# Softmax weights and tokens turned by transposing transfers of 16-bit halves instead of TensorE

## The chip, the cores and the metric

The kernel runs on one core of one Trainium2 chip. Its engines are called as in the profile: PE (TensorE, the matmuls; PEld is its weight load), DVE (VectorE), ACT (ScalarE), POOL (GpSimd) and SP (SyncE, which issues every transfer here). The metric is the time of one execution on the device in microseconds (us). Three runs of the kernel before took 473.75, 475.15 and 475.65 us, so the median is 475.15 us.

## The reference

Sparse attention over 4 batches, 8 heads, 768 positions and 64 channels is followed by a mixing block on the joined heads (512 channels). All data is 32-bit float.

```python
def _attn_ref(q, k, v):
    block, window = (32, 16)
    k_sum = k.reshape(B, H, nb, block, D).max(axis=3)       # 24 block keys
    v_sum = v.reshape(B, H, nb, block, D).mean(axis=3)      # 24 block values
    scores_l = scale * q @ k.T           # kept where |i - j| < 16
    scores_s = scale * q @ k_sum.T + log(block)
    a = softmax(concatenate([scores_l_m, scores_s]))
    return a @ concatenate([v, v_sum])

def _moe_ref(x, w_theta, w_tok_r, w_tok_i, w_ch):
    theta = x @ w_theta
    zr, zi = x * cos(theta), x * sin(theta)
    y = w_tok_r @ zr + w_tok_i @ zi      # over the positions of a batch
    u = x + y
    return u + maximum(u @ w_ch, 0.0)
```

## The kernel before

Each batch has six tiles of 128 positions. For one tile, `att_tile` multiplies queries with 24 block keys and 94 neighbouring keys for each of two groups of 64 queries (118 scores a row, L1609). `att_half`, called twice for four heads each, takes the maximum on DVE (L1622), the exponential on ACT (L1626), turns the four 128x118 blocks of weights on PE into PSUM (L1629, tile `p`), copies them to SBUF (`pt`, by the helper at L1466) and multiplies them with the values (L1635, tile `av`). DVE or ACT divides by the sums into `xn`, which holds a tile of tokens by position.

`turn_tile` then turns the four 128x128 blocks of `xn` on PE (L1657, tile `t`), copies them to their place in `x`, which holds the turned tokens of a whole batch, and splits them in a leading part `xh` (L1466) and a rest `xl` (L1472), since PE multiplies in a shorter format, three products for one. `theta_tile` multiplies with `w_theta` (L1689) and takes cosine and sine (L1697 to L1712); products with the tokens go to `w` and `zb`, split into `zq`. When a batch has its six tiles, `mix_step` adds up the token mixing in two halves `h` of six steps `s`: for batch 0 at L1732, after that at L1767. At the last step DVE adds `x` to the sums in place (L1778) and the result `u` goes to DRAM (`u_scratch`). After all batches the pools of the attention are given back, and `out_unit` loads `u`, splits it, multiplies with `w_ch` (L1809) and stores the output.

The weights come as halves of 64-bit numbers that `load_f64` converts on ACT, DVE and POOL while batch 0 runs (L1513 to L1522).

The order of everything is written out in the table ORDER: the letters name the engine (P, A, V, G, S for PE, ACT, DVE, POOL, SP) and the numbers are steps from one recorded operation to the next. Each engine works through its own part of the list in order and waits for what an operation reads and for its buffers. SP issues all transfers in this order too, so that one that waits holds those behind it. Attention of a batch is interleaved with the mixing of the batch before. Buffers that matter here: `xn` has 2, `pt` 1, `e` 2, the values `v` 4, `x` 2.

Of the kernel before, what the change touches and what calls it, by code (L numbers as in the profile page):

```python
# [1913 lines left out]
```

## Time and profile before

| | |
|---|---|
| median of three runs | 475.15 us |
| the profiled execution | 473.4 us |
| its span, first to last instruction | 471.6 us |
| PE busy | 452.2 us, 96% |
| DVE busy | 326.2 us, 69% |
| ACT busy | 267.0 us, 57% |
| POOL busy | 125.9 us, 27% |
| moved by transfers | 62.16 MB, 132 GB/s in the mean |

All numbers of the trace are from the one profiled execution; 1.8 us of its time lie outside the span. Busy is the time in which an engine worked on at least one instruction, so the durations of instructions that overlap add up to more than it. Matmuls overlap by their drain: how long one kept PE is read from its start to the next start.

### The profile page before, as it was taken

The numbers are of one execution on the slowest core, as the hardware profiler recorded it, in microseconds if no ns is written. First come the engines' busy times: TensorE is split into PE (matmuls) and PEld (weight loads), VectorE is DVE, ScalarE is ACT, GpSimd is POOL, SyncE is SP. The second block draws the span as 40 slices with busy tenths as digits, with TensorE's granted clock in tenths as the row PEclk, the third lists the DMA queues.
The fourth block names the chain that finished last, engine by engine and source line by source line (L and its number), as shares of the span: only waits on it lengthen the run. The fifth ranks groups of instructions, "written<-read, shape, count | busy, mean of one in ns | idle before, by whom it ended". The sixth has DMA issues, their size and how long they took to land.

```text
span 471.6 us, 10324 instructions
## 1 busy us (share of the span) xinstructions
PE 452.2 (96%) x3904; PEld 384.5 (82%) x3904; DVE 326.2 (69%) x999; ACT 267.0 (57%) x568; POOL 125.9 (27%) x160
## 2 busy tenths in 40 slices
PE   2999899999999999999999899999999999999997
PEld 1487667778888888888888688888888889999996
DVE  5899999999899776747668665434756695333354
ACT  2499999977588785736467846647754230010010
POOL 3235453434133122132123332322110220130310
PEclk9999999999999999999999999999999999999999
DMA  8988645334116351251082204020101651473663
GB/s 318 363 276 286 222 153 170 99 122 124 58 34 199 122 158 45 71 179 33 21 286 78 75 1 125 22 70 2 35 24 44 208 161 68 133 247 110 207 200 121
DMA packets 34226, 62.16 MB, mean 132 GB/s; under 512 B 3968, under 2 KB 16000, under 8 KB 34176
## 3 DMA queue, kind: packets, MB, share of 16 engines
...
HBM read 48.90 MB, written 12.58 MB: 130 GB/s over the span
## 4 chain that ended last, share of the span: by engine, by line
PE 80%; ACT 6%; DVE 5%; DMA 3%; issue 3%; POOL 1%; SPq 1%; ACTq 0%; POOLq 0%; DVEq 0%
PE m L1767 29%; PE c L1809 14%; PE t L1689 11%; PE m L1732 8%; PE av L1635 5%; PE p L1629 4%; PE s L1609 4%; PE t L1657 2%; PE m L1497 2%; PE av L1548 1%; DVE f L1522 1%; ACT e L1626 1%; SPq L1463 1%; ACT pt L1466 1%; ACT L1711 1%
## 5 line engine op out<-in xcount | busy, mean ns | idle before, releaser
L1767 PE MATMUL m<-wt,zq 128*128 128x512 f32 x864 | 162.2, 340 | 0.0
L1767 PEld LDWEIGHTS m<-wt,zq 128*128 128x128 f32 x864 | 133.3, 188 | 17.9
L1626 ACT ACTIVATE e<-e,st 128x118 f32<-128x118 f32 x192 | 66.6, 389 | 14.5 <-DVE st L1622 13.2
L1809 PE MATMUL c<-cuh,wth 128*128 128x384 f32 x256 | 65.7, 338 | 0.0
L1689 PE MATMUL t<-wth,xh 128*128 128x512 f32 x192 | 61.4, 401 | 0.0
L1732 PE MATMUL m<-wt,zq 128*128 128x512 f32 (+1 forms) x288 | 56.8, 344 | 0.1
L1622 DVE CUSTOM_DVE_ANT_0 e<-s,cs 128x118 f32<-128x118 f32 x192 | 46.3, 272 | 11.9 <-PE p L1629 6.5
L1732 PEld LDWEIGHTS m<-wt,zq 128*128 128x128 f32 x288 | 43.9, 189 | 7.1 <-DVE zq L1472 0.7
L1466 ACT CAST cuh<-cu 128x384 fp32r<-128x384 f32 x19 | 9.5, 513 | 68.2 <-DMA cu<-u_scratch 65.6
L1809 PEld LDWEIGHTS c<-cuh,wth 128*128 128x128 f32 x256 | 45.9, 188 | 0.5
L1809 PE MATMUL c<-cul,wth 128*128 128x384 f32 x128 | 43.3, 338 | 0.2 <-DVE cul L1472 0.2
L1814 DVE SCALAR_TENSOR_TENSOR cu<-c,cu 128x384 f32<-128x384 f32 x32 | 17.5, 554 | 34.4 <-PE c L1809 24.2
L1635 PEld LDWEIGHTS av<-v,pt 118*64 118x64 f32 x768 | 27.0, 137 | 17.1 <-issue 9.0
L1472 POOL TENSOR_TENSOR zq<-w,zq 128x512 fp32r<-128x512 f32 x14 | 19.4, 1387 | 73.3 <-ACT zq L1466 43.1
L1689 PEld LDWEIGHTS t<-wth,xh 128*128 128x128 f32 x192 | 33.5, 188 | 6.7 <-issue 0.5
L1689 PE MATMUL t<-wth,xl 128*128 128x512 f32 x96 | 37.8, 394 | 0.0
L1635 PE MATMUL av<-v,pt 118*64 118x65 f32 x768 | 33.6, 227 | 3.7 <-DMA v<-vg 2.5
L1697 ACT ACTIVATE w<-t,bmagic 128x512 f32<-128x512 f32 x24 | 16.5, 686 | 32.2 <-PE t L1689 20.7
L1629 PE MATMUL p<-cs,e 128*118 128x128 f32 x192 | 30.4, 281 | 0.9 <-ACT e L1626 0.9
L1472 POOL TENSOR_TENSOR zq<-zb,zq 128x512 fp32r<-128x512 f32 (+1 forms) x19 | 22.9, 1211 | 27.0 <-ACT zq L1466 20.1
L1472 POOL TENSOR_TENSOR cul<-cu,cuh 128x384 fp32r<-128x384 f32 x14 | 15.1, 1094 | 55.8 <-ACT cuh L1466 33.1
L1472 POOL TENSOR_TENSOR xl<-x,xh 128x512 fp32r<-128x512 f32 x11 | 14.4, 1310 | 53.8 <-DVE xh L1466 33.1
...
## 6 DMA issues: line engine op xcount, KB each, us to landing
...
q<-qg SPq DMA_DIRECT2D x24, 256.0 KB, 3.9
cu<-u_scratch SPq DMA_DIRECT2D x32, 192.0 KB, 2.8
out<-cu SPq DMA_DIRECT2D x32, 192.0 KB, 2.0
...
u_scratch<-x SPq DMA_DIRECT2D x16, 256.0 KB, 3.7
wt<-wtr SPq DMA_DIRECT2D x6, 512.0 KB, 6.3
wt<-wti SPq DMA_DIRECT2D x6, 512.0 KB, 7.2
```

The lines of the kernel that those rows point to most:

```text
L1472: op(f"VG tt {n}", lambda e: V[e].tensor_tensor(dst(), src(), hi().bitcast(F32), op=ALU.subtract), reads, writes)
L1609: mm("s" if len(parts) == 1 else "s0", [lambda p=p, g=g, h=h, c=c, kk=kk: nc.tensor.matmul(sc[h].get()[ROW[g], p, c], q.get()[ROW[h], p, R ...
L1622: op("V ttr", lambda eng, n=n: nc.vector.tensor_tensor_reduce(e.get()[:, n], sc[n % 2].get()[:, 2 * a + n // 2], mask(m), -SCALE, 3.0e38, ...
L1626: op("A exp", lambda eng, n=n: nc.scalar.activation(e.get()[:, n], e.get()[:, n], AF.Exp, bias=st.get()[:, n:n + 1], scale=-1.0), [(st, n) ...
L1629: mm("tr", [lambda n=n: nc.tensor.transpose(tp.get()[:NK, n], e.get()[:, n], ident()) for n in range(NH)], [e, (cs, "ident")], [tp])
L1635: mm("av", [lambda n=n, g=g: nc.tensor.matmul(xa.get()[ROW[g], n], t.get()[:, n, ROW[g]], v[g].get()[:NK, NH * a + n], start=True, stop=Tr ...
L1689: calls = [lambda t=t, xx=xx, k=k, c=c: nc.tensor.matmul(th.get(), xx.get()[:, c], w_th[c].get()[:, k], start=(c == 0 and t == 0), stop=(c ...
L1697: op(f"A psumb {DM}", lambda e: nc.scalar.activation(r(), th.get(), AF.Identity, bias=bmagic.get(), scale=1.0 / TWO_PI), [th, bmagic], [R])
L1732: nc.tensor.matmul(acc, zk(k, r, c), w_t[s, r, th].get()[:, kw], start=(clear and s == r == t == 0), stop=(s == NT - 1 and r == 1 and t == ...
L1767: nc.tensor.matmul((ma[c].get(), half(2, c)())[th], zk(k, r, c), w_t[s, r, th].get()[:, kw], start=(s == r == t == 0 and (th == 0 or c == 0)),
L1809: calls = [lambda t=t, k=k, uu=uu, c=c, co=co, acc=acc: nc.tensor.matmul(acc.get(), w_ch[c].get()[:, k, co * P:(co + 1) * P], uu.get()[:, ...
L1814: op(f"V ttp {HT}", lambda e, co=co, acc=acc: nc.vector.scalar_tensor_tensor(u.get()[:, co], acc.get(), 0.0, u.get()[:, co], ALU.max, ALU. ...
```

## The change

From tile `DT` = 6 on, that is for batches 1 to 3, the turning matmuls and the copies out of PSUM give way to `turn_words`: a copy parts the 32-bit numbers in two planes of 16 bits (`un`, the operation called part), one transposing transfer on SP's queue turns 128 rows of 1024 such halves, eight blocks of 128x128, from SBUF to SBUF (`ut`), and a second copy joins the halves (join). Either copy may go to POOL, ACT or DVE. For the softmax weights, 118 wide, the ten columns that fill a block up are zeroed first. Batch 0 is turned by PE as before.

The turned tokens have no buffer for a whole batch any more. Each tile of `x` is stored to `u_scratch` (512 runs of 512 bytes), loaded again in `mix_step` as `ux`, added to and stored a second time. Eight buffers `zx` of 2 KB a partition serve `un`, `ut`, the tile of tokens and the first loads of values; `ux` has four. ORDER is new from end to end; one line of it stands for the rest.

```diff
-S+98
+S+104
...
-TUNE = dict(XT=1, XB=2, WB=1, TB=1, XNB=2, XHB=2, FB=2, FC=2, QB=2, VB=4, KN=2, ZQ=8, ZS=11, EB=2, PC=4, WU=40)
+TUNE = dict(XT=1, WB=1, TB=1, XNB=2, XHB=2, FB=2, FC=2, QB=2, VB=4, KN=2, ZQ=8, ZB=11, ZX=8, UX=4, DT=6, EB=2, PC=4, WU=40)
...
+    def turn_words(n, w, src, reads, dst, writes):
+        un = Ref(tpool, [P, 2, n, P], U16, tag="zx", bufs=K["ZX"])
+        ut = Ref(tpool, [P, 2, n, P], U16, tag="zx", bufs=K["ZX"])
+        if w < P:
+            op("GV set 1", lambda e: V[e].memset(un.get()[..., w:], 0), [], [(un, "pad")])
+        op(f"GAV part {2 * n * w}", lambda e: copy(e, un.get()[..., :w], src().bitcast(U16).rearrange("p n (w k) -> p k n w", k=2)),
+           reads, [(un, "data")])
+        op("S turn 128 2048", lambda e: nc.sync.dma_start(
+            ut.get().rearrange("p k n t -> p (k n) t"), un.get().rearrange("p k n w -> p (k n w)"), transpose=True), [un], [ut])
+        op(f"GAV join {2 * n * P}", lambda e: copy(e, dst().bitcast(U16).rearrange("w n (t k) -> w k n t", k=2), ut.get()[:w]), [ut], writes)
...
-        tp = bank("p", [P, NH, P])
-        mm("tr", [lambda n=n: nc.tensor.transpose(tp.get()[:NK, n], e.get()[:, n], ident()) for n in range(NH)],
-           [e, (cs, "ident")], [tp])
         t = Ref(apool, [NK, NH, P], tag="pt", bufs=K["TB"])
-        op(f"AV psum {NH * P}", lambda e: copy(e, t.get(), tp.get()[:NK]), [tp], [t])
+        if b * NT + i < K["DT"]:
+            tp = bank("p", [P, NH, P])
+            mm("tr", [lambda n=n: nc.tensor.transpose(tp.get()[:NK, n], e.get()[:, n], ident()) for n in range(NH)],
+               [e, (cs, "ident")], [tp])
+            op(f"AV psum {NH * P}", lambda e: copy(e, t.get(), tp.get()[:NK]), [tp], [t])
+        else:
+            turn_words(NH, NK, e.get, [e], t.get, [t])
...
+        x = Ref(tpool, [P, NC, P], tag="zx", bufs=K["ZX"])
...
+        else:
+            turn_words(NC, P, lambda: xn[b, i].get().rearrange("p h d -> p (h d)").rearrange("p (c d) -> p c d", d=P), [xn[b, i]], x.get, [x])
+        hi_op(x_h.get, x.get, DM, [x], [x_h])
+        lo_op(x_l.get, x.get, x_h.get, DM, [x, x_h], [x_l])
+        dma(lambda: u_dram[b][:, :, i * P:(i + 1) * P].rearrange("c p t -> p c t"), x.get, NC * P, P * 4, [x], [("ud", (b, i))])
...
+                u = Ref(tpool, [P, 512], tag="ux", bufs=K["UX"])
+                part, row = (lambda u=u, n=n: u.get()[:, :n]), (lambda th=th, ch=ch: u_dram[b, ch][:, TT[th]])
+                dma(part, row, P, n * 4, [("ud", (b, t)) for t in range(i0, i0 + n // P)], [u])
+                op(f"V ttp {n}", lambda e, part=part, acc=acc: nc.vector.tensor_tensor(part(), acc(), part(), op=ALU.add), [areg], [u])
+                dma(row, part, P, n * 4, [u], [("ur", (b, ch, th))])
```

Three places show what moves. The first is DVE at the end of batch 0's mixing, where it adds the tokens to the last sums (L1778 before, L1848 now; `m` is a bank of sums, L1622 and L1684 are the maxima). Before, the last of batch 0's additions is its instruction 443, with 88 maxima ahead of it:

```order
L1648 TENSOR_TENSOR xn_2182<-av_2077,st_1837 128x256
L1778 TENSOR_TENSOR x_400<-m2_1595,x_400 128x256
L1622 ISA e_2059,st_2060<-s1_1954,cs_170 128x118
L1622 ISA st_2060 128x1
L1778 TENSOR_TENSOR x_400<-m1_1472,x_400 128x256
L1778 TENSOR_TENSOR x_400<-m0_1516,x_400 128x512
L1560 TENSOR_REDUCE vt_2221<-f_2196 128x16
L1778 TENSOR_TENSOR x_400<-m1_1472,x_400 128x256
```

Now it is instruction 494, with 97 maxima ahead of it:

```order
L1706 RECIPROCAL st_2037<-st_2037 128x4
L1713 TENSOR_TENSOR xn_2347<-av_2369,st_2037 128x256
L1610 TENSOR_REDUCE vt_2016<-f_2390 128x8
L1610 TENSOR_REDUCE vt_2016<-f_2357 128x16
L1516 CAST zq_2414<-w_2255 128x512
L1684 ISA e_2423,st_2424<-s1_2330,cs_120 128x118
L1684 ISA st_2424 128x1
L1848 TENSOR_TENSOR ux_2426<-m1_1712,ux_2426 128x256
```

DVE has 51 more instructions ahead of that addition than before. The second place is PE at the last tile of the last batch, where its tokens are turned and multiplied with `w_theta`. Before, PE turns them (`t` from `xn`) in the midst of the mixing:

```order
L1767 MATMUL m0_4533<-wt200_1060,zq_4557 128x512
L1767 MATMUL m2_4534<-wt201_1702,zq_4557 128x256
L1657 MATMUL t_4710<-cs_170,xn_4675 128x128 x4
L1767 MATMUL m1_4576<-wt110_856,zq_4374 128x512
L1767 MATMUL m2_4534<-wt111_1529,zq_4374 128x256
```

Now mixing goes on to the first theta matmul of that tile, which reads `xh` and `xl`:

```order
L1835 MATMUL m0_4608<-wt300_734,zq_4755 128x512
L1835 MATMUL m2_4609<-wt301_1830,zq_4755 128x256
L1835 MATMUL m0_4608<-wt300_734,zq_4805 128x512
L1835 MATMUL m2_4609<-wt301_1830,zq_4805 128x256
L1757 MATMUL t_4849<-wth0_80,xh_4821 128x512 x2
L1757 MATMUL t_4849<-wth0_80,xl_4834 128x512
```

The turn has left PE's list; between the tile's last product with the values and this theta matmul PE has 12 mixing matmuls, the 12 theta matmuls of the tile before and 18 more mixing matmuls. The third place is SP in the attention of the last batch, with loads of queries and values (`q`, `v`) and stores of `u`. Before:

```order
L1463 DMA u_scratch<-x_1651 128x512
L1463 DMA v_3737<-vg 96x520
L1463 DMA q_4103<-qg 128x512
L1463 DMA q_4124<-qg 128x512
L1463 DMA v_3674<-vg 96x520
L1463 DMA v_3665<-vg 96x520
L1463 DMA v_3737<-vg 96x520
```

Now (`zx` from `zx` is a turn, `u_scratch` from `zx` the store of a turned tile):

```order
L1513 DMA v_3750<-vg 96x520
L1674 DMA_TRANSPOSE zx_4519<-zx_4444 128x8x128
L1674 DMA_TRANSPOSE zx_4524<-zx_4459 128x8x128
L1513 DMA v_3616<-vg 96x520
L1513 DMA v_3799<-vg 96x520
L1674 DMA_TRANSPOSE zx_4604<-zx_4535 128x8x128
L1674 DMA_TRANSPOSE zx_4668<-zx_4549 128x8x128
L1513 DMA u_scratch<-ux_4425 128x512
L1513 DMA u_scratch<-ux_4264 128x256
L1674 DMA_TRANSPOSE zx_4691<-zx_4551 128x8x128
L1674 DMA_TRANSPOSE zx_4742<-zx_4698 128x8x128
L1513 DMA u_scratch<-zx_4633 128x4x128
```

The turns stand in the same queue as the loads of values, which wait behind them.

## Rows read from the trace of the kernel before

**Rows 1.** The head of the profile's page: the span, and each engine's busy time, its share of the span and its instructions.

```profile
span 471.6 us, 10324 instructions
PE 452.2 (96%) x3904; PEld 384.5 (82%) x3904; DVE 326.2 (69%) x999; ACT 267.0 (57%) x568; POOL 125.9 (27%) x160
```

**Rows 2.** The chain that ended last, its shares of the span by engine.

```profile
PE 80%; ACT 6%; DVE 5%; DMA 3%; issue 3%; POOL 1%; SPq 1%; ACTq 0%; POOLq 0%; DVEq 0%
```

**Rows 3.** Busy time of each engine (and its instructions) in stretches of the span, in us; behind them the granted clock, the share of the DMA engines and GB/s.

```profile
core 0: us, PE busy (x) PEld busy (x) DVE busy (x) ACT busy (x) POOL busy (x), PEclk, DMA share, GB/s
0.00:30.00 30.00, 20.68 (x216) 12.68 (x217) 22.62 (x75) 13.91 (x30) 9.54 (x15) 1.00 0.91 316
30.00:60.00 30.00, 27.43 (x440) 21.86 (x441) 29.13 (x99) 29.09 (x64) 13.34 (x13) 1.00 0.80 269
60.00:100.00 40.00, 38.30 (x283) 29.21 (x282) 38.72 (x112) 37.08 (x77) 15.87 (x24) 1.00 0.45 141
100.00:148.00 48.00, 48.00 (x468) 41.40 (x468) 43.33 (x152) 34.85 (x83) 15.55 (x23) 1.00 0.30 96
148.00:154.00 6.00, 6.00 (x75) 5.03 (x74) 5.86 (x14) 4.64 (x14) 1.65 (x2) 1.00 0.53 176
154.00:340.00 186.00, 183.67 (x1669) 155.29 (x1668) 117.31 (x416) 119.65 (x246) 47.18 (x66) 1.00 0.27 83
```

**Rows 4.** The timeline of PE in a piece of batch 2: start in us, duration in us, engine, line, operation, output from input. `p` from `cs,e` are turns of softmax weights, `t` from `cs,xn` turns of tokens, `m` the mixing, `t` from `wth` the theta matmuls (12 of them from 212.64 us to 215.50).

```profile
204.31 0.65 PE L1629 MATMUL p<-cs,e 128*118 128x128 f32 x4
204.72 4.43 PE L1767 MATMUL m<-wt,zq 128*128 128x512 f32 x24
209.08 0.69 PE L1635 MATMUL av<-v,pt 118*64 118x65 f32 x16
...
210.66 0.65 PE L1629 MATMUL p<-cs,e 128*118 128x128 f32 x4
211.15 0.60 PE L1657 MATMUL t<-cs,xn 128*128 128x128 f32 x4
211.51 1.29 PE L1767 MATMUL m<-wt,zq 128*128 128x512 f32 x6
212.64 0.69 PE L1689 MATMUL t<-wth,xh 128*128 128x512 f32 x2
...
215.50 0.73 PE L1767 MATMUL m<-wt,zq 128*128 128x512 f32 x3
```

**Rows 5.** Groups of instructions by line, engine, operation and shape: count, busy us, mean ns of one, and the idle time of the engine before them with what ended it.

```profile
L1626 ACT ACTIVATE e<-e,st 128x118 f32<-128x118 f32 x192 | 66.6, 389 | 14.5 <-DVE st L1622 13.2 <-DVE st L1641 0.6
...
L1622 DVE CUSTOM_DVE_ANT_0 e<-s,cs 128x118 f32<-128x118 f32 x192 | 46.3, 272 | 11.9 <-PE p L1629 6.5 <-PE s L1609 4.8 <-issue 0.5
...
L1635 PE MATMUL av<-v,pt 118*64 118x65 f32 x768 | 33.6, 227 | 3.7 <-DMA v<-vg 2.5 <-DVE xn L1648 0.5 <-ACT pt L1466 0.3
...
L1711 ACT ACT_TABLE_LOAD x20 | 25.7, 1283 | 0.3
...
L1472 POOL TENSOR_TENSOR zq<-w,zq 128x512 fp32r<-128x512 f32 x14 | 19.4, 1387 | 73.3 <-ACT zq L1466 43.1 <-DVE zq L1466 30.2
...
L1466 ACT COPY pt<-p 118x512 f32<-118x512 f32 x31 | 17.9, 577 | 12.6 <-PE p L1629 9.1 <-issue 2.5 <-PE av L1635 0.9
...
L1648 DVE TENSOR_TENSOR xn<-av,st 128x256 f32<-128x256 f32 x38 | 16.0, 421 | 1.2
...
L1472 DVE TENSOR_TENSOR zq<-zb,zq 128x512 fp32r<-128x512 f32 x22 | 15.6, 716 | 0.7 <-ACT zq L1466 0.5
...
L1466 POOL COPY k<-kn 128x188 f32<-128x188 f32 x38 | 14.9, 404 | 22.3 <-PE s L1609 22.1
...
L1466 ACT CAST zq<-zb 128x512 fp32r<-128x512 f32 x24 | 14.5, 619 | 1.7 <-PE m L1732 1.4 <-DVE zb L1719 0.3
...
L1466 DVE COPY pt<-p 118x512 f32<-118x512 f32 x17 | 11.6, 684 | 6.0 <-ACT k L1466 4.0 <-PE p L1629 2.0
...
L1542 DVE TENSOR_REDUCE ks<-kn 128x48 f32<-128x1536 f32 x6 | 10.5, 1746 | 0.0
L1517 POOL TENSOR_SCALAR f<-f 128x512 f32<-128x512 f32 x15 | 9.9, 663 | 26.9 <-ACT f L1513 17.9 <-DVE f L1515 8.9
...
L1472 DVE TENSOR_TENSOR xl<-x,xh 128x512 fp32r<-128x512 f32 x13 | 8.9, 687 | 0.3 <-ACT xh L1466 0.2
...
L1641 DVE RECIPROCAL st<-st 128x4 f32<-128x4 f32 x48 | 8.2, 172 | 2.9 <-ACT st L1639 2.4
...
L1466 DVE CAST zq<-zb 128x512 fp32r<-128x512 f32 x12 | 5.1, 424 | 0.0
...
L1466 POOL COPY v<-q 24x512 f32<-24x512 f32 x4 | 3.7, 930 | 4.2 <-ACT q L1566 4.2
...
L1466 ACT CAST zq<-zb 128x256 fp32r<-128x256 f32 x5 | 2.0, 401 | 0.4 <-DVE zb L1719 0.4
```

**Rows 6.** The timeline of DVE at the last addition for batch 0, columns as in rows 4.

```profile
151.33 0.41 DVE L1778 TENSOR_TENSOR x<-m,x 128x256 f32<-128x256 f32 x1
```

**Rows 7.** Issues of transfers by line: output from input, count, KB each, and the median time from issue to landing in us.

```profile
q<-qg SPq DMA_DIRECT2D x24, 256.0 KB, 3.9
...
out<-cu SPq DMA_DIRECT2D x32, 192.0 KB, 2.0
...
wth<-wth SPq DMA_DIRECT2D x4, 512.0 KB, 7.8
```

More of the change, by code (lines that the diff above doesn't have):

```diff
@@ new lines @@
+P-9,-339
+S+111
+A+1
+S+31,+236
+V-32
+A+4,-1
+P-349,+1,+1
+S+212,+166
+V-403,+100
+A+274,-12
+P-37,+79
+G-285
+S+227,-77
+V-149,+1,+14
+G+212
+V-225
+A+204,+1,-204
+G+1
+V+12,+192,+79
+P-44,+12
+V+44,+3,-58
+S-183
+P+149,+1
+V+77
+A-242
+P+166,+1
+V+72,+1
+A+4,+2
+V+9,-56
+A+46,-2
+V-242
+A+209
+P+37
+V-47
+A+59
+P-399,+351
+A-43
+V-197,+31
+A+255
+V-3
+A+4
+V-255
+G+166
+A+91
+S-285,+312,-240
+P+243
+V-318,+198
+S+66
+V-263,+275
+A-77,+41
+P-351
+V+352,+1
+P+35
+A-77
+V+121
+P-78
+V-211
+S+107
@@ new lines @@
+A+45,+193
+V-182
+P-84
+V+29
+P+11
+S-204
+V+401
+P-119
+V-77,+42,-1
+A-81,-97
+V+138
+A-308
+V+1
+A+530
+G-562,+204,+360
+S-475,+454
+G+23
+A-197,+14,+1
+G-85
+P+115,-568,+1
+V+453
+A-338
+P+411
+G-410
+A+377,+34,-73
+P+40,+76
+V+127
+A-202
+V-378,+418
+S-20,-353,+532,-178
+A+22,+1
+V-421,+1
+S+653
+V-652,+1
+P+599,-154
+V+155
+A-225
+G+1
+A-42
+S-253
+V+493,+28
+S-31
+P-164
+A+1
+G+216
+A-20
+P-185
+V+182
+P-223,+1,+1,+68
+V-406,+577,+68,-84
+S-278
+V+11
+S+252
+V-16
+G+88,-617
+V+1
+G+617
+V-326
@@ new lines @@
+G+1
+P+1
+S+14
+P+91
+A-193
+S+50
+V+1
+A+1,+37
+S-225
+V+25
+S+507
+A-256
+S+258,-344
+V-53
+G+159
+A-21
+G+110
+V-247,+88,+1,+103
+A+54
+G+3,-92
+S+2,+84
+P-365,+2,-1
+G+9,+163
+S+337,-523
+A+236
+P-217
+A+15
+G+243
+P-40
+V+1
+P-50,+1
+V+50,+1,+103
+A+4
+V-3
+S-350
+A+247
+S+1
+A+53
+V-260,+101,+210
+P-325
+V+116,+393
+S+9
+P-349,+1
+A+1
+V+138,-54,+53
+A+4,+15
+S-27,-43
+V+50
+A+4
+G+51,-190
+V+339,-187,-151,+1
+S-146,+494,-18,-205
+A+11,-88,+91
+P-309,-7,+2,+4
+V+220
+A-216
+G+308,-91
+P+51
@@ new lines @@
+V-153
+P+195
+V+1
+G+14
+A+53,-15
+V-51
+P-178
+V-21,+260,-15
+G+7
+A-207,+206,-3
+P-225
+G+278
+P-276
+V+175,+63
+A-14
+P-36
+S-183
+V-2
+A+128
+S-127,+7
+A+178,+39
+P+49
+V+1,+1
+A-147
+V+148
+P-281,+2
+A+241,+42,+51
+V-202
+P+2,+1
+V-130,+184,+91,-269,-3
+S+379,-254
+G-113,-6
+P+1,+1,+1
+S+254
+A+13,-46
+S-27
+V-186
+A+165
+S-184
+V+237
+S-15
+P-92,+1,-116
+G+221,-216
+V+269
+P-277,+5,+4
+S+243
+G-79,+38
+P+1
+V+63,+3,-2
+A+4,+1,-18
+S-272
+A+129
+G+1
+V+1
+A+1
+S+103
+A+38,+18,-158
+S+50
+P-170
@@ new lines @@
+V+9
+P-2
+G+302
+V-138,-50
+A+88
+V+1,-88,-112
+S-20,+316,-270
+A+239
+G+36
+P-309,+4
+V+166
+G+1
+A+137,-87
+V-12
+P+13,+89
+G+57
+V-106
+A-39
+S+82
+A-184,+157
+V-265,+211,+1
+G+1
+S+1
+V+85
+G-298
+P+159,+1,+1,+1
+V+155,-54
+S+2
+V+34
+P-307,+4
+V+112
+A+55
+G+84
+S+2
+A+104
+G-189
+A-159
+P-7,+4
+G+4
+P-11,+9
+A+298
+P-294
+V+308
+A+4
+V-5
+P-318
+V+317,-13
+S-284,+141,-144,-3
+A+310
+V-156
+A+1,+1
+V+1,+132,-131
+A+136,+13,+37
+V-49,-92,+1,+1
+P-215
+G+351,-30
+S-105
+A+33,+53,+1
+P-53
+G+15
@@ new lines @@
+S-55
+G+1
+V+55,+1
+P+31
+A-131,+80
+P+1
+A+1
+P+44
+V-43
+A+1,+17
+V-56
+P+83
+V-82
+P+2,+1,+1,+1
+V-50
+A+51
+V+1,+1
+S-66,-263,+377,+48,-103,-319
+A+375
+V+1
+S+2,+41,+6
+P-23
+V-25
+P+28,-1
+A-77
+P+52
+A-51
+V+1
+P+51,+1,+1
+V-51,+1,-2
+A+53
+V+1,+1,+1
+A+1
+P+20,+2,-3,+2
+A+26
+V-46,+2,+1
+P+19,+1
+V+17,-39,+40,+6
+P-23,+2
+S+2
+V+1
+P-4,+2
+V+11,-6,+3
+S+53,+1
+V+1,-38
+S+69,+42
+G-72
+V+1
+S+38,-33
+V+1
+S+15,+47
+G-107
+A+69
+G+1,-24
+V+1,-7,+1
+P-52,+1,+1,+4,-3,+4,+1,+1
+V+44,+6
+P-47,+2
@@ L1362 @@
+P-25
+A+30
+P-13,-10,+1
+V+1
+P+9,-17,+18,+1,-18
+V+1,+18
+S+11,-22,-210
+A+233
+P-236
+A+230
+V+7
+P+19,-12,-6
+V-7,-223
+S+199
+G+27
+P+23,-12,+1,+12
+S-39,+6,-215,+252
+P-15,+3
+S-241
+V+2
+S+1,+253
+P-14,+8
+V-11,+15
+S-14,+19
+A-2
+S+5
+A-2
+V-9
+S+1
+P-22,+13,+1
+V+1
 S+1
```

2290 lines of the change are left out of this document (976 added, 1314 removed).

## Prediction

> **What bounds the kernel now.** I read the engines' busy shares first: PE is busy 452.2 of 471.6 us, every other engine at most 69% [rows 1]. Then the chain that ended last: 80% of it is PE [rows 2], so what PE no longer does can shorten the span, and what the others get to do counts only where PE comes to wait for them. Where that may be is in the table by stage [rows 3]. Through the first 100 us PE stands idle 9.3, 2.6 and 1.7 us, while DVE is busy 29.1 of 30 and 38.7 of 40 us: there DVE, which also converts the weights, sets the pace. From 100 to 154 us PE has no idle time; from 154 to 340 us it loses 2.3 us, and DVE and ACT are busy 63% and 64%, POOL 25%. The engine that gains most work by the change, POOL, has the most room. The granted clock is full throughout.
>
> **What PE sheds.** Three groups of four turning matmuls per tile, in 18 of the 24 tiles: 36 groups for the weights, 18 for the tokens. A group's own duration in the trace holds a drain that lies under the next work, so I take start to next start [rows 4]: 0.41 and 0.49 us for the weights, mean 0.45, and 0.36 for the tokens. 36 x 0.45 + 18 x 0.36 = 22.7 us. With it go 54 copies out of PSUM (29 on ACT, 25 on DVE by the two orders).
>
> **What the others get.** Each turn needs a copy that parts the halves (944 or 1024 elements of 16 bits), one transfer, and a copy that joins them: 108 copies, by the new order 53 on ACT, 11 on DVE, 44 on POOL. The trace has no such copy, so I go by what it has for 32 bits [rows 5]. ACT: 256 elements take 401 ns and 512 take 619; on that line it is 0.99 and 1.05 us (twice 619 ns at most). 53 of them are 55 us, less 29 x 0.58 for the copies that go and 6 x 1.28 for table loads (34 stand in the new order against 40): +30 us on an engine idle for 205. DVE: between 0.85 (twice its cast of 512, 424 ns) and 1.4 us (twice its subtraction, 716); I take 1.2, which 11 times is less than the 25 x 0.68 that it sheds. POOL: from 1.3 (twice its clamp, 663 ns) to 2.8 (twice its subtraction, 1387 ns); I take 1.7, from its two copies, 404 ns for 188 elements and 930 for 512, as the same kind of operation. 44 x 1.7 = 75 us on 126 of 471.6: hidden in total, but both copies stand in chains that PE waits for.
>
> **The new order ahead of batch 1.** The front of the program is where cover is thin. DVE's last addition for batch 0 is its instruction 443 in the old order and 494 in the new one (the rows from DVE that the change shows). Ahead of it stand, net, 9 more maxima (0.35 us with their read-outs), 2 more reductions of 1.75 us, 9 more weight steps and some 10 more casts, subtractions and products, by their durations 18 us; DVE's durations overlap a little (up to there they sum to 163 us where it is busy 137), so 15.5 us of busy time. In the trace that addition starts at 151.3 us [rows 6]; DVE has been busy 137.0 us by then (the first five rows of rows 3, less 2.6 us from the addition on) and idle 14.3. With 15.5 us more it starts at 161 us if DVE's idle time shrinks to 8.3 (what it has in the first 60 us), at 167 if not. PE's own work ahead of it is about the same in both orders (137 and 138 us), so PE idles 8 to 15 us longer there; I take 11. Work that DVE has done early could be given back only where PE waits later, and that is 2.3 us.
>
> **The transfer.** 54 transposes of 256 KB from SBUF to SBUF, all on SP's queue. No row shows one. By size the nearest row is the load of 256 KB, 3.9 us to landing; the ends are 2.0 (192 KB out) and 7.8 us (512 KB in) [rows 7]. I take 4 us. What it must fit into I counted through the new order of PE: the work, by the starts in rows 4, between the matmuls that end a chain's source and those that use its result. For the 36 weight turns that is 19 to 37 us; the chain is four maxima, an exponential of 0.39, a table load, two copies (2.1 to 3.5) and the transfer: 9 to 11 us, covered even at twice the transfer. For the 18 token turns it is 7.0, 8.3, 8.3, 9.3, 10.1, 10.9, 11.3, 11.9, 12.4 us and nine from 13.2 up. (One of the 8.3 is the place that the change shows from PE: 15 pairs of mixing matmuls at 0.36 us and 12 theta matmuls at 0.24.) Their chain is two steps at 0.17, the product 0.42, two copies 2.1, a cast 0.42, the rest 0.69: 4.0 us on the fast engines, 5.6 where one leg is POOL's and with hand-overs. With a transfer of 4 us the shortfalls are 2.6 + 1.3 + 1.3 + 0.3 = 5.5 us; at 2.0 us 0.6, at 7.8 us 31.3. Behind a transpose that waits, SP's queue holds loads of v and q and stores of u, as the rows from SP show; PE waits for loads of v 2.5 us in all now [rows 5], the loads are issued ahead by four buffers, and I add nothing.
>
> [...]
>
> **DRAM.** Tokens go out per tile (24 stores of 256 KB) and come back for the addition (32 loads of 256 or 128 KB): about 12.6 MB more on 62, where the DMA engines are busy 27% to 53% after 100 us [rows 3]. Mixing covers them, tens of us for each half. Taken as nothing; a load that is late keeps a mixing accumulator taken, and PE then waits for up to one landing, 4 us.
>
> **Sum.** The profiled execution took 473.4 us; the median of the runs is 475.15, 0.4% above it, which I leave out. 473.4 - 22.7 + 11 + 5.5 = 467 us.
>
> **Rivals.** *A, the forecast*, 458 to 472 us: the PE work goes, part of it is lost ahead of batch 1 and in the shortest token chains. Chance 0.48.
> *B, everything is covered*: 473.4 - 22.7 = 451. For it: from 154 us on, DVE and ACT have a third of their time free. Against: DVE's longer list ahead of batch 1. 0.08.
> *C, the transfer is slow* (slower than before): one transpose lands in 6 us or more, because it moves elements of two bytes or holds SP while it is issued, and the token chains then hold PE at their theta matmuls. At 7.8 us: 473.4 - 22.7 + 11 + 31.3 = 493. It decides from about 5.5 us on, where the shortfalls reach the 11.7 us that are left of the gain. For it: no row shows the operation, and 18 chains in a row leave no way round it. Against: the row of 256 KB. 0.31.
> *D, the copies hold it* (the gain is spent): a POOL copy at 2.8 us lengthens a token chain by 1.1 us a leg, and 27 of the 44 lie in 110 us of PE's work, where POOL would then be busy nine tenths. About 8 us more: 475. Against: its plain copies are cheaper than that. 0.13.
>
> **Numbers.** The runs shown lie within 0.4%, so 0.5% either way (472.8 to 477.5) can't be told from no change. Faster: A and B, 0.56. Same: most of D and a little of C, 0.11. Slower: the rest, 0.33. The range goes from B, 450, to 506, which is C with a transfer of nearly 9 us. A's own range is 458 to 472.
>
> **What would show it.** PE busy near 430 us. The last addition for batch 0 near 163 us instead of 151; if it comes by 153, the step on DVE's list is wrong and B is nearer. Transposes landing in about 4 us; at 6 or more, idle time of PE ahead of theta matmuls of tens of us in all (C). POOL's 16-bit copies near 1.7 us; near 2.8, D.

## The result: 0.6% slower, and the profile after

The changed kernel took 478.13 us (median of 17 runs, 476.18 to 481.91) where the kernel before took 475.42 beside it: ratio 1.0059, 95% interval 1.0037 to 1.0082. The forecast was 467 us. Ratios, here and below, leave out two disturbed executions, 480.53 us of e1 and 1447.64 us of e12, which the medians count. The head of the page of the changed kernel answers to [rows 1]:

```profile
span 475.9 us, 10196 instructions
PE 436.3 (92%) x3688; PEld 362.7 (76%) x3688; DVE 331.9 (70%) x1011; ACT 297.7 (63%) x587; POOL 169.8 (36%) x210
```

PE did shed work: 15.9 us less busy time. But PE's idle time, span less busy, grew from 19.4 to 39.6 us. So 20.2 us of new idle time ate 15.9 us of saved work, and the span grew by 4.3. The table by stage, in the stretches of [rows 3] and one more, says where (busy us of each engine; then clock, DMA share, GB/s):

```profile
core 0: us, PE busy (x) PEld busy (x) DVE busy (x) ACT busy (x) POOL busy (x), PEclk, DMA share, GB/s
0.00:30.00 30.00, 19.66 (x246) 12.22 (x250) 21.48 (x73) 14.51 (x35) 5.63 (x12) 1.00 0.95 318
30.00:60.00 30.00, 24.53 (x402) 18.57 (x394) 26.96 (x101) 25.72 (x57) 6.85 (x7) 1.00 0.63 208
60.00:100.00 40.00, 33.90 (x273) 24.99 (x272) 37.22 (x116) 39.31 (x82) 18.11 (x24) 1.00 0.72 214
100.00:148.00 48.00, 44.11 (x379) 36.18 (x378) 45.27 (x152) 42.46 (x85) 16.04 (x25) 1.00 0.76 184
148.00:154.00 6.00, 5.68 (x72) 4.59 (x70) 3.46 (x6) 4.91 (x8) 2.16 (x2) 1.00 1.16 288
154.00:340.00 186.00, 177.20 (x1559) 145.76 (x1560) 127.06 (x434) 137.52 (x268) 92.52 (x112) 1.00 0.78 179
340.00:475.00 135.00, 131.27 (x777) 120.41 (x775) 70.47 (x135) 33.29 (x58) 28.50 (x30) 1.00 0.49 153
```

Up to 100 us PE is idle 21.9 us (13.6 before); from 100 to 154 us 4.2 (none before), from 154 to 340 us 8.8 (2.3 before). ACT is busy 42.46 of 48 us from 100 to 148 us (34.85 before). The last addition for batch 0 [rows 6] starts at 174.18 us, not at 151.33:

```profile
174.18 0.42 DVE L1848 TENSOR_TENSOR ux<-m,ux 128x256 f32<-128x256 f32 x1
```

The new operations, by shape (part writes `zx` from `e` or `xn`, join writes `pt` or `zx` from `zx`; count, busy us, mean ns, idle time ahead and what ended it), and the product `zb`, which no edit touches:

```profile
L1516 POOL COPY pt<-zx 118x1024 uint16<-118x1024 uint16 x18 | 25.9, 1439 | 26.9 <-DMA zx<-zx 17.8 <-PE av L1700 9.1
L1787 DVE TENSOR_TENSOR zb<-xn,w 128x512 f32<-128x512 f32 x30 | 24.4, 818 | 0.5 <-ACT w L1780 0.4
...
L1516 ACT COPY pt<-zx 118x1024 uint16<-118x1024 uint16 x16 | 21.7, 1354 | 2.4 <-DMA zx<-zx 2.3
...
L1516 ACT COPY zx<-e 128x944 uint16<-128x944 uint16 x20 | 19.4, 977 | 0.2
...
L1516 POOL COPY zx<-zx 128x1024 uint16<-128x1024 uint16 x8 | 12.3, 1534 | 8.4 <-DMA zx<-zx 8.4
...
L1516 POOL COPY zx<-e 128x944 uint16<-128x944 uint16 x11 | 10.9, 989 | 10.9 <-ACT e L1688 7.3 <-issue 3.6
...
L1516 ACT COPY zx<-xn 128x1024 uint16<-128x1024 uint16 x10 | 10.4, 1042 | 3.5 <-DVE xn L1713 3.5
...
L1516 POOL COPY zx<-xn 128x1024 uint16<-128x1024 uint16 x7 | 7.8, 1109 | 7.0 <-ACT xn L1711 3.5 <-issue 2.4 <-DVE xn L1713 1.1
...
L1516 DVE COPY pt<-zx 118x1024 uint16<-118x1024 uint16 x2 | 1.5, 757 | 0.8 <-DMA zx<-zx 0.8
```

The transposes on SP's queue (ns min, median, max that one holds the queue; then the first and last start in us), and the median us to landing, which answers to [rows 7]:

```profile
L1674 SPq DMA_TRANSPOSE zx<-zx x54: 1231/1232/4018, 90.6 to 359.4; - x54
```

```profile
zx<-zx SPq DMA_TRANSPOSE x54, 3.5
```

A transpose lands in 3.5 us (4 forecast) and holds SP's queue for 1.23. The first is issued at 90.6 us; 8.3 us of the new idle time lie ahead of 100 us, nearly all of it before any turn by transfer has begun.

### The profile page after: what moved, and what is told of

Its sections match the earlier page's. It is cut to its first block, busy times and chain, and to the rows that moved or that the text cites. A ratio compares the mean times of both kernels' runs of the same rounds, so it can differ in the third digit from the quotient of the medians.

```text
span 475.9 us, 10196 instructions
## 1 busy us (share of the span) xinstructions
PE 436.3 (92%) x3688; PEld 362.7 (76%) x3688; DVE 331.9 (70%) x1011; ACT 297.7 (63%) x587; POOL 169.8 (36%) x210
## 2 busy tenths in 40 slices
DMA packets 108578, 88.89 MB, mean 187 GB/s; under 512 B 61936, under 2 KB 88304, under 8 KB 108528
## 3 DMA queue, kind: packets, MB, share of 16 engines
q1 hardware_dynamic: 108528, 88.24, 69.0%
## 5 line engine op out<-in xcount | busy, mean ns | idle before, releaser
L1688 ACT ACTIVATE e<-e,st 128x118 f32<-128x118 f32 x192 | 65.6, 388 | 17.0 <-DVE st L1684 13.6
L1684 DVE CUSTOM_DVE_ANT_0 e<-s,cs 128x118 f32<-128x118 f32 x192 | 46.4, 273 | 10.9 <-PE s L1658 4.4
L1700 PE MATMUL av<-v,pt 118*64 118x65 f32 x768 | 33.2, 227 | 10.5 <-ACT pt L1516 3.1
L1757 PEld LDWEIGHTS t<-wth,xh 128*128 128x128 f32 x192 | 33.9, 188 | 10.5 <-ACT xh L1516 1.8
L1757 PE MATMUL t<-wth,xl 128*128 128x512 f32 x96 | 38.4, 400 | 2.2 <-POOL xl L1522 1.5
L1567 POOL TENSOR_SCALAR f<-f 128x512 f32<-128x512 f32 (+1 forms) x16 | 10.7, 671 | 74.9 <-DVE f L1565 38.1
L1516 POOL COPY pt<-zx 118x1024 uint16<-118x1024 uint16 x18 | 25.9, 1439 | 26.9 <-DMA zx<-zx 17.8
L1522 POOL TENSOR_TENSOR cul<-cu,cuh 128x384 fp32r<-128x384 f32 x16 | 16.6, 1049 | 50.8 <-ACT cuh L1516 24.4
L1522 POOL TENSOR_TENSOR zq<-zb,zq 128x512 fp32r<-128x512 f32 (+1 forms) x19 | 24.5, 1291 | 15.6 <-issue 6.6
L1787 DVE TENSOR_TENSOR w<-xn,w 128x512 f32<-128x512 f32 x18 | 13.9, 774 | 18.9 <-ACT w L1780 18.9
```

What stands on the lines that cost most here:

```text
L1516: (nc.scalar.copy if e == "ACT" else V[e].tensor_copy)(dst, src)
L1522: op(f"VG tt {n}", lambda e: V[e].tensor_tensor(dst(), src(), hi().bitcast(F32), op=ALU.subtract), reads, writes)
L1684: op("V ttr", lambda eng, n=n: nc.vector.tensor_tensor_reduce(e.get()[:, n], sc[n % 2].get()[:, 2 * a + n // 2], mask(m), -SCALE, 3.0e38, ...
L1688: op("A exp", lambda eng, n=n: nc.scalar.activation(e.get()[:, n], e.get()[:, n], AF.Exp, bias=st.get()[:, n:n + 1], scale=-1.0), [(st, n) ...
L1700: mm("av", [lambda n=n, g=g: nc.tensor.matmul(xa.get()[ROW[g], n], t.get()[:, n, ROW[g]], v[g].get()[:NK, NH * a + n], start=True, stop=Tr ...
L1757: calls = [lambda t=t, xx=xx, k=k, c=c: nc.tensor.matmul(th.get(), xx.get()[:, c], w_th[c].get()[:, k], start=(c == 0 and t == 0), stop=(c ...
```

## Experiments

Three theories stood at the start. *Issue*: transposes hold up SP's queue and its loads. *Copies*: 108 copies of halves fill ACT and DVE. *Order*: the new ORDER, whatever turns the tiles. All results in one table; PE busy and idle (span less busy) are of the profiled execution, "b0" is the start of the last addition for batch 0. PE's busy time holds the granted clock too: it was at 0.5 of full speed for 2.9 us in the changed kernel's trace (0.999 in the mean of the span), for 14.8 in e1's (0.986) and for 35.2 in e3's (0.967).

| run | median us | ratio to before (95%) | PE busy | PE idle | b0 |
|---|---|---|---|---|---|
| before | 475.42 | | 452.2 | 19.4 | 151.3 |
| after | 478.13 | 1.0059 (1.0037-1.0082) | 436.3 | 39.6 | 174.2 |
| e1 | 476.66 | 1.0013 (0.9982-1.0044) | 440.5 | 33.7 | 173.6 |
| e2 | 470.42 | 0.9887 (0.9835-0.9939) | 438.5 | 29.9 | 169.0 |
| e3 | 511.63 | 1.0770 (1.0727-1.0813) | 452.4 | 61.5 | 197.7 |
| e4 | 507.09 | 1.0660 (1.0624-1.0696) | 468.9 | 35.4 | 174.7 |
| e5 | 499.58 | 1.0481 (1.0433-1.0529) | 455.6 | 41.3 | 182.7 |
| e6 | 483.33 | 1.0161 (1.0132-1.0190) | 442.9 | 37.0 | 178.6 |
| e7 | 473.55 | 0.9959 (0.9933-0.9985) | 442.9 | 30.5 | 170.1 |
| e8 | 494.84 | 1.0400 (1.0369-1.0430) | 460.9 | 33.3 | 164.2 |
| e9 | 468.54 | 0.9879 (0.9832-0.9925) | 436.8 | 29.4 | 167.0 |
| e10 | 467.57 | 0.9849 (0.9813-0.9885) | 439.2 | 26.4 | 168.0 |
| e11 | 471.34 | 0.9914 (0.9884-0.9945) | 444.4 | 25.3 | 170.1 |
| e12 | 480.82 | 1.0111 (1.0082-1.0141) | 440.8 | 38.4 | 174.8 |
| e13 | 475.64 | 1.0008 (0.9989-1.0027) | 440.2 | 35.2 | 174.9 |
| e14 | 470.33 | 0.9895 (0.9857-0.9933) | 440.8 | 27.6 | 172.0 |
| e15 | 481.44 | 1.0125 (1.0095-1.0155) | 454.9 | 24.7 | 159.1 |
| e16 | 475.34 | 1.0009 (0.9993-1.0024) | 453.3 | 20.2 | 156.6 |
| e17 | 478.01 | 1.0071 (1.0039-1.0102) | 436.5 | 39.6 | 173.2 |
| e18 | 470.90 | 0.9911 (0.9876-0.9946) | 436.6 | 29.9 | 166.8 |

**What the turning itself costs (e1, e2).** First the transposes alone go, then the strided copies too.

```diff
-            ut.get().rearrange("p k n t -> p (k n) t"), un.get().rearrange("p k n w -> p (k n w)"), transpose=True), [un], [ut])
+            ut.get().rearrange("p k n t -> p (k n t)"), un.get().rearrange("p k n w -> p (k n w)")), [un], [ut])
```

> The 54 transposing transfers become plain transfers of the same 256 KB between the same buffers (weights and tokens of batches 1 to 3 are then not turned); copies, order and everything else as in the changed kernel. Theory 'issue' (a transpose holds SP's queue for 1.23 us against 0.36 for a plain transfer, so loads behind it come late): 464 to 470 us, and PE's idle time falls by 6 to 12 us. Theory 'copies' (the 108 copies of 16-bit halves fill ACT and DVE): within 2 us of the changed kernel, 476 to 480. Theory 'order' (the new order has more of DVE's work ahead of batch 0's last addition, whatever turns the tiles): that addition stays at 169 us or later, and the time within 3 us of the changed kernel.

```diff
-        op(f"GAV part {2 * n * w}", lambda e: copy(e, un.get()[..., :w], src().bitcast(U16).rearrange("p n (w k) -> p k n w", k=2)),
+        op(f"GAV part {2 * n * w}", lambda e: copy(e, whole(un)[..., :w], src()),
...
-        op(f"GAV join {2 * n * P}", lambda e: copy(e, dst().bitcast(U16).rearrange("w n (t k) -> w k n t", k=2), ut.get()[:w]), [ut], writes)
+        op(f"GAV join {2 * n * P}", lambda e: copy(e, dst(), whole(ut)[:w]), [ut], writes)
```

> As the run with plain transfers, and both copies of each turn are of whole 32-bit numbers, half as many elements (again not turned). Theory 'copies': at least 6 us below the run with plain transfers, and PE waits less for tile pt and for the parts of the tokens. Theory 'issue': within 2 us of the run with plain transfers. Theory 'order': batch 0's last addition still starts at 167 us or later, 15 us or more behind the kernel before, although nothing of the turning costs much any more; the time is at best 460.

In e1 the transfer lands in 2.9 us and holds SP for 0.47 (time to landing; then ns that one holds the queue):

```profile
zx<-zx SPq DMA_DIRECT2D x54, 256.0 KB, 2.9
```

```profile
L1674 SPq DMA_DIRECT2D zx<-zx x54: 465/471/791, 92.0 to 356.8; - x54
```

That is worth 0.5%, some 2 us, where "issue" expected 8 or more: a part, not the cause. (PE's idle time fell by 5.9 us, near what "issue" asked, but its busy time rose by 4.2 with the same matmuls and a mean granted clock of 0.986 instead of 0.999.) Copies of whole numbers, not halves, are worth 6 us more, as "copies" said; 108 copies at 0.42 to 0.72 us in the mean and 54 transfers are still there. The addition still starts at 169.0 us, as "order" said, and 29.9 us of idle time are left, 10.5 more than before.

**The list alone, first attempts (e3 to e5).** ORDER is replaced from end to end, operations stay.

```diff
-S+104
-V+1,+1,+1,+1,+1
+S+1,+1,+110
+A+1
...
```

> The same operations as in the changed kernel (108 copies, 54 transposes, tokens by way of DRAM); only the table ORDER is another one, with other engines for some copies (POOL has 59 of them, ACT 30, DVE 19, where they were 44, 53 and 11). It was found by following the list with the durations of the traces and keeping what ends earlier. DVE has 368 operations ahead of batch 0's last addition, 397 in the changed kernel and 354 before. Theory 'order': the addition starts at 150 to 158 us and the time is 445 to 458. Theory 'copies' or 'issue' (the turning costs more than it saves, in any order): 468 us or more, with PE idle ahead of the values' and theta's matmuls.

For e4 and e5 `DT=24` and `DT=12` go with it:

> All 24 tiles turned by TensorE (DT = 24), tokens still by way of DRAM, and a table ORDER found in the same way from the order of the kernel before. Theory 'order': 460 to 470 us, so that a better list gains for TensorE's turns too, and the transfers gain 12 to 20 us more beside it. If the way by DRAM costs something itself: above 473. Theory 'the turning costs more than it saves': no slower than the run with the new list and transfers.

> Batch 0 and 1 turned by TensorE, batches 2 and 3 by transfers (DT = 12), ORDER found in the same way. PE has 8 us more work than with transfers from batch 1 on, the front 12 turns fewer. Theory 'order': within 5 us of the run with the new list and the same turns, 445 to 460. Theory 'copies' (turns hurt where DVE also converts the weights): at least 5 us below that run.

All three came out 37 to 54 us above the expectation: no theory was tested, the way of finding lists was wrong. The traces say a good part of why. In e3 DVE is busy 384.7 us, 53 more than in the changed kernel, though its operations there, at the changed kernel's mean durations, would add up to 3.5 us less; `zb`'s product takes 915 ns, 699 before. PE is busy 16.1 us more with the same matmuls, its clock at 0.5 for 35.2 us. Timelines of DVE and POOL in e3:

```profile
139.92 1.52 DVE L1906 SCALAR_TENSOR_TENSOR f<-wt,f 128x256 int32<-128x256 int32 x1
141.47 1.37 DVE L1908 SCALAR_TENSOR_TENSOR f<-wt,f 128x256 uint32<-128x256 uint32 x1
142.88 1.23 DVE L1852 CAST wt<-f 128x256 fp32r<-128x256 f32 x1
144.15 0.43 DVE L1858 TENSOR_TENSOR wt<-f,wt 128x256 fp32r<-128x256 f32 x1
```

```profile
139.69 1.47 POOL L1858 TENSOR_TENSOR zq<-zb,zq 128x512 fp32r<-128x512 f32 x1
141.11 1.51 POOL L1852 COPY pt<-zx 118x1024 uint16<-118x1024 uint16 x1
142.55 1.41 POOL L1858 TENSOR_TENSOR zq<-zb,zq 128x512 fp32r<-128x512 f32 x1
```

Each of the first three DVE operations ends 0.15 to 0.28 us after the POOL operation under which it began (141.44 after 141.16, 142.84 after 142.62, 144.11 after 143.96); in the changed kernel their means are 430, 449 and 390 ns. In all of e3, 93 of DVE's products, sums, shifts, casts and copies between SBUF and SBUF began with more than 0.3 us of a POOL operation still to run, and all 93 ended after it. POOL is busy 228.1 us in e3, 169.8 in the changed kernel.

**With the exclusion (e6 to e8).** The same, with that taken into the account (e7 with `DT=9`, e8 with `DT=24`):

```diff
-S+104
-V+1,+1,+1,+1,+1
+S+128,-81
+V+82,+1,+1
...
```

> The operations of the changed kernel again and only another ORDER, found as in e3, but following the list so that DVE's copies, casts, subtractions and shifts between SBUF and SBUF and POOL's operations exclude each other, as e3 and e4 showed. Copies by engine: ACT 50, POOL 35, DVE 23. DVE has 378 operations ahead of batch 0's last addition. Theory 'order with the exclusion': 455 to 468 us, DVE busy below 345, zb's product near 0.75 us (0.82 in the changed kernel, 0.92 in e3). Theory 'the turning costs more than it saves': 473 or more.

> As e6 with the transfers from tile 9 on (DT = 9), so that the first half of batch 1, the tiles turned while DVE still converts weights, stays on TensorE: 3.9 us more of PE's work, 18 copies of 16-bit halves fewer. 360 operations of DVE ahead of batch 0's last addition. If the copies hurt only in the front: 450 to 463 and below e6. If it is the order alone: e6 plus 0 to 4 us.

> As e6 with all tiles turned by TensorE (DT = 24), tokens by way of DRAM. 339 operations of DVE ahead of that addition. Theory 'order': 463 to 474 us, 5 to 15 above e6: turning by transfer is then worth that much under one way of ordering. If turning by transfer is worth nothing under any order: no slower than e6.

Closer, but still late, and e8 by most. What the exclusion was to do came: in e6 DVE is busy 333.8 us and `zb`'s product takes 0.71. e8 is 11.5 us above e6, as "order" said; between e4 and e3 it was the other way round, 4.5 us. e7 is the first list that beats the kernel before, by 0.4%. e6 against e7 can't be read for the turns of batch 1: the two lists differ everywhere. In all three PE idles 4 to 7 us more in the first 30 us than before. Its first scores are no later (11.2 to 12.4 us, 14.2 before); what has moved back is most of the 40 warm-up matmuls, which multiply zeros and stood at 9.0 us and after.

**With slack (e9 to e11).** Hand-overs are taken longer than they are, and the first loads stay in place. The warm-up matmuls don't, though it was meant: they begin at 38.1 us in e9, 9.7 in the changed kernel.

```diff
-S+104
-V+1,+1,+1,+1,+1
+V+71
+S+33
...
```

> The changed kernel's operations once more and another ORDER alone. This time the list was followed with the durations and overlaps measured in the traces so far (a DVE operation starts 0.08 us before the one ahead of it ends, one of ACT 0.10), DVE and POOL excluding each other, hand-overs taken longer than they are so that chains get slack, and the loads of the first 35 us and the warm-up matmuls left in their places. By the same reckoning the kernel before comes to 471 and the changed one to 479. Reckoned: 453; the lists so far came out 12 to 21 us later than reckoned, so 455 to 470 if order is what the change lost by; 474 or more if the turning costs what it saves under any order.

> The same way of ordering with the transfers from tile 9 on. Reckoned: 450, so 452 to 468; against e9 it tells whether the turns of the first half of batch 1 are worth having (then up to 4 us above e9) or cost (then below e9).

> The same way of ordering with the transfers from tile 12 on, that is with batch 1 turned by TensorE. Reckoned: 452, so 454 to 470; 3.9 us more of PE's work than from tile 9 on, and no 16-bit copy before about 150 us, where ACT and DVE are full in the changed kernel. If these copies are what hurts, it is at least as fast as e10.

e9 is the answer to "order": the changed kernel's own operations take 468.5 us in another list, 1.2% less than the kernel before and 1.8% less than the changed one. The list differs in sequence, and 342 of its 2460 operations are on another engine. Its stages:

```profile
core 0: us, PE busy (x) PEld busy (x) DVE busy (x) ACT busy (x) POOL busy (x), PEclk, DMA share, GB/s
0.00:30.00 30.00, 15.23 (x188) 7.80 (x188) 21.71 (x73) 13.01 (x29) 5.27 (x12) 0.94 0.94 310
30.00:60.00 30.00, 27.30 (x359) 20.83 (x359) 28.80 (x100) 27.27 (x58) 10.91 (x9) 0.94 0.89 285
60.00:100.00 40.00, 35.94 (x350) 27.39 (x348) 39.08 (x123) 38.86 (x83) 16.15 (x26) 0.96 0.75 200
100.00:148.00 48.00, 47.02 (x409) 39.14 (x408) 46.63 (x162) 45.79 (x91) 11.14 (x17) 1.00 0.70 167
148.00:154.00 6.00, 6.00 (x66) 5.34 (x66) 5.86 (x14) 5.96 (x11) 0.98 (x1) 1.00 1.34 275
154.00:340.00 186.00, 183.27 (x1617) 150.66 (x1616) 142.99 (x461) 136.91 (x276) 70.04 (x90) 1.00 0.76 183
```

Up to 100 us PE is idle 21.5 us, as long as in the changed kernel; from 100 to 340 us 3.7 instead of 13.0. It is no faster for having less on ACT there: ACT and DVE are as full. The granted clock below 1.00 in the first rows is one of 0.5 for 10 us in all; PE had stood idle 1.6 and 1.7 us shortly before it fell. That this lowered it isn't shown: in the changed kernel PE stood idle 2.3 us at 167 us with the clock at 1.00. e10, with the first half of batch 1 left on TensorE, is not told apart from e9, and is the fastest measured by its median; e11, with all of batch 1 on TensorE, comes out between them and the kernel before. So the turns of batch 1 do not hurt by being there, as far as lists that differ everywhere can tell.

**Engines or sequence (e12, e13), and two controls (e14, e15).** e12 changes 43 letters alone, e13 places alone; e14 is e10's list searched on, e15 `DT=24` in the way of e9.

```diff
-A-581,+582,+18
+A-581
+V+582
+A+18
...
```

> The changed kernel's ORDER in its own sequence; only 43 of the 108 copies of 16-bit halves are given to another engine (ACT 53, DVE 26, POOL 29, where it was 53, 11, 44; which tile's copy goes where changes more than the numbers do). Reckoned as before: 9 us below the changed kernel. Theory 'copies' (the loss is copies that wait on a full engine): 468 to 473. Theory 'sequence': at most 3 us below the changed kernel.

```diff
-S+104
-V+1,+1,+1,+1,+1
+V+71,+3
+S+30
...
```

> Every operation on the engine that the changed kernel gives it, the sequence alone another. Reckoned: 20 us below the changed kernel; lists came out some 10 later than reckoned, so 464 to 472 by the theory 'sequence'. Theory 'copies': 475 or more, since the copies stay on the engines where they are. DVE has 398 operations ahead of batch 0's last addition, as many as in the changed kernel (397): if that addition comes at 170 us or later here too and the kernel is faster all the same, its lateness is not the loss.

> The list of e10 searched on, transfers from tile 9 on. Reckoned 2 us below e10: 463 to 468, the fastest of all if that holds.

> The same way of ordering with all tiles turned by TensorE and the tokens by way of DRAM: what e9, e10 and e14 are to be compared with, if one asks for the turning alone. Reckoned: 470, against 458 for e9 and 454 for e14. Theory 'the transfers gain once the list suits them': 474 to 486, 8 to 16 above e9. Theory 'the gain of e9 is the way of ordering, not the transfers': within 4 us of e9.

Other engines for 43 copies alone gain nothing (1.0111): "copies on full engines" falls as the sole cause, and with it the reckoning of 9 us. The sequence alone gains 0.5%, less than its theory asked; 475.6 us lies in the range that "copies" gave. Both together gave 1.8% (e9). I take it that another engine helps if the place in its queue is chosen with it, but no run moves all 342 of e9's letters alone. In e13 the addition comes at 174.9 us, later than in the changed kernel, and the time is 2.5 us less; in e12 at 174.8 with 2.7 us more. Its lateness is not the loss. e14 missed: 470.3, not below e10, so differences of 2 us are beyond this way of finding lists. e15 is the control that counts: the same way of ordering with TensorE's turns takes 481.4 us, 12.9 more than e9. (e16, below, runs the same operations as e15 in the old list's sequence in 475.3 us: the old list is better made than mine.)

**DRAM, front and rest (e16 to e18).** e16 keeps the kernel before's sequence on PE, DVE, ACT and POOL and takes the tokens by way of DRAM (`DT=24`); e17 and e18 re-order the changed kernel ahead of 100 us and after it.

```diff
-TUNE = dict(XT=1, WB=1, TB=1, XNB=2, XHB=2, FB=2, FC=2, QB=2, VB=4, KN=2, ZQ=8, ZB=11, ZX=8, UX=4, DT=6, EB=2, PC=4, WU=40)
+TUNE = dict(XT=1, WB=1, TB=1, XNB=2, XHB=2, FB=2, FC=2, QB=2, VB=4, KN=2, ZQ=8, ZB=11, ZX=8, UX=4, DT=24, EB=2, PC=4, WU=40)
...
```

> The kernel before with one part of the change: tokens go to DRAM tile by tile and come back for the additions. All tiles are turned by TensorE (DT = 24); PE, DVE, ACT and POOL keep the kernel before's sequence, and only SP's stores and loads are put in. The prediction took this way as free: 474 to 477. If the loads that come back hold batch ends up: 479 to 484 (the reckoning says 4 us more).

```diff
-S+104
-V+1,+1,+1,+1,+1
+G+71,-65
+V+68
...
```

> The changed kernel with another sequence (and 76 other engines) in the first 100 us alone, as the trace counts; 439 of PE's 579 operations, from the end, stay where they are. Reckoned 5 us below the changed kernel. If the loss sits in the front, where PE idles 8 us more before the first transpose has landed: 468 to 474. If it sits later: within 3 us of the changed kernel.

```diff
-P+40,+76
+P+40
+S+282
+P-206
...
```

> The other way round: the changed kernel's first 100 us kept, another sequence and other engines after them. Reckoned 22 us below the changed kernel, lists came out 10 to 13 later than reckoned: 466 to 472 if the loss sits after 100 us, 475 or more if it sits in the front.

The way by DRAM is free (1.0009). This re-ordering of the front gains nothing; keeping the front and re-ordering the rest gains nearly all of e9. But e17 does not show that the front costs nothing: up to 100 us PE idles 20.9 us in it, against 21.9 in the changed kernel, 15.2 in e16 and 13.6 before. In the other lists, those that turn all tiles on PE among them, it is 18.4 to 27.0, so that loss goes with the new lists and not with the turning, and no run wins it back. The changed kernel's rows for 100 to 180 us and for 180 to 340, then those of e18:

```profile
100.00:180.00 80.00, 70.78 (x624) 57.83 (x623) 71.49 (x224) 69.87 (x140) 29.20 (x39) 1.00 0.76 184
180.00:340.00 160.00, 156.21 (x1386) 128.70 (x1385) 104.31 (x368) 115.02 (x221) 81.52 (x99) 1.00 0.80 182
```

```profile
100.00:180.00 80.00, 76.04 (x704) 61.82 (x703) 74.37 (x242) 71.76 (x136) 23.97 (x32) 1.00 0.73 189
180.00:340.00 160.00, 157.77 (x1369) 130.23 (x1368) 118.40 (x392) 127.60 (x234) 57.02 (x77) 1.00 0.77 181
```

From 100 to 180 us PE waits 9.2 us in the changed kernel and 4.0 in e18, with ACT and DVE fuller, not emptier, in e18. From 180 to 340 us POOL has given 24 us of work to DVE and ACT in e18. From 100 to 180 us batch 1 is turned, and DVE converts weights until 160. PE's waits in the changed kernel from 100 to 340 us, by what ended them (us in total, times, longest; `pt` are turned weights, `xh` and `xl` the parts of turned tokens, `ux` an addition at the end of mixing):

```profile
PE s L1658 <- issue: 2.3, 1, 2.3
PE av L1700 <- ACT pt L1516: 2.0, 4, 0.9
PE m L1800 <- DVE ux L1848: 1.2, 1, 1.2
PE av L1700 <- issue: 1.1, 1, 1.1
PE t L1757 <- DVE xh L1516: 1.1, 1, 1.1
PE m L1800 <- DVE wt L1522: 0.9, 1, 0.9
PE av L1700 <- DVE xn L1713: 0.9, 2, 0.7
PE t L1757 <- DVE xl L1522: 0.7, 2, 0.5
PE av L1700 <- POOL pt L1516: 0.6, 1, 0.6
```

No line holds a fifth of the 13.0 us that PE is idle there: many small gaps, not one place. The longest stands under "issue", which names nothing, but the timeline around it tells more:

```profile
165.47 1.36 POOL L1516 COPY pt<-zx 118x1024 uint16<-118x1024 uint16 x1
165.66 1.65 DVE L1787 TENSOR_TENSOR w<-xn,w 128x512 f32<-128x512 f32 x1
...
166.73 1.76 POOL L1516 COPY zx<-zx 128x1024 uint16<-128x1024 uint16 x1
...
167.43 1.55 DVE L1787 TENSOR_TENSOR zb<-xn,w 128x512 f32<-128x512 f32 x1
...
168.91 0.27 DVE L1684 CUSTOM_DVE_ANT_0 e<-s,cs 128x118 f32<-128x118 f32 x1
...
169.31 0.08 DVE L1684 DVE_READ_ACCUMULATOR2_ANT st<- 128x1 f32 x1
...
169.49 1.19 PE L1658 MATMUL s<-k,q 64*64 64x118 f32 x32 [2.33 <-issue]
```

By the semaphores PE's scores wait here for DVE to have taken the maxima of earlier ones. These stand behind two products of DVE that last 1.65 and 1.55 us, where their medians are 0.69, each begun under a join on POOL. An estimate from these numbers: without the joins the maxima would have come 1.8 us earlier. By this estimate the exclusion of DVE and POOL, which the prediction left out, makes most of the longest wait; for the others that isn't shown.

## Why the prediction was wrong, step by step

- **What bounds the kernel**: right as far as it goes. PE is the busiest engine in every run, 88% to 96% of the span. (Idle time is defined as span less busy, so that the two add up proves nothing.)
- **PE sheds 22.7 us**: the work was sized right, the saving was not. Taking each kind of matmul at its median from start to start, the work fell from 420.1 to 397.0 us. Busy time fell by only 15.9. Each gap leaves the drain of the matmul ahead of it (0.16 to 0.19 us; a mixing matmul of 512 columns lasts 0.395 us and the next starts after 0.232) without cover: 48 gaps instead of 17, 7.9 us instead of 3.3. That explains 4.6 of the missing 7.2 us. The other 2.6 are starts that came later than their median without PE falling idle, 31.1 us in all instead of 28.5. The prediction took start to next start for the very reason that drains lie under the next work, and then let them lie there while adding waits.
- **The front, +11**: mis-sized, and its mechanism was not the loss. It and PE's saving together made the sign wrong. DVE's added work was right: it is busy 153.4 us ahead of the addition, 152.5 by the forecast's sum. But DVE itself waits, 20.8 us by then instead of 8.3 to 14.3, and the addition came 23 us late. PE's idle time up to 180 us grew by 17.5, of it 8.3 ahead of 100 us and 9.2 after. Yet e13 has the addition as late and is faster, and PE nowhere waits for it: the one wait for an addition of batch 0 is 1.2 us at 129 us, for one of the early ones. The prediction read the place of one instruction as the place of the loss.
- **ACT, "+30 us on an engine idle for 205"**: the wrong view, with joins mis-sized. Of the 205 us 104 lie after 340 us, where 5 of ACT's 53 copies run; from 100 to 180 us ACT had 19.9 of 80 free and gets 19 copies. Joins on ACT took 1.35 us, not 1.05; parts were right (0.98 and 1.04). e2 puts the price of halves against whole numbers, on all engines, at 6 us. That a full ACT is the loss isn't shown: it is busy 69.9 us in that stretch, and 71.8 in e18, where PE waits less.
- **POOL**: a part took 0.99 to 1.11 us, a join 1.44 to 1.53, under the forecast's 1.7; rival D's 2.8 did not come. What was left out is that DVE's products took longer under POOL's copies: 1.65 and 1.55 us at 165 to 169 us above, 0.69 in the median.
- **The transfer, 4 us, +5.5**: right on landing: 3.5 us, against 2.9 for the plain one in e1. The term of 5.5 us was too large: PE waits for the parts of turned tokens ahead of theta 1.8 us in all (another 2.6 us of such waits lie in batch 0, whose tokens PE turns itself). For turned weights, taken as covered, it waits 2.9. Rival C falls.
- **SP's queue, nothing**: 1.23 us of holding instead of 0.47 cost, with the slower landing, some 2 us (e1), just clear of the noise.
- **DRAM, nothing**: right (e16).
- **The sum**: forecast -22.7 + 16.5 = -6.2; measured -15.9 + 20.2 = +4.3 us of span. Of the miss of 10.5 us, 6.8 are PE's term and 3.7 the idle time. That the idle time came so near is luck: of the 20.2 us, 8.3 lie ahead of 100 us, 9.2 from there to 180, 2.7 after, and only 4.7 are waits for turned tiles.
- **The sign**: it hangs on ORDER. Shown: the same operations take 468.5 us in another list, 470.9 with the first 100 us kept (e9, e18); turning by transfer is worth 12.9 us where both are ordered in one way (e15). The changed list gives that away, 8.3 us ahead of 100 us and the rest after it in many small waits; only the latter was won back (e18). Open: what single moves of that list do it, and what makes the front slow. e12 and e13 only say that neither 43 copies on other engines nor another sequence does it alone.
